# Gate and value products by seven block products instead of eight, with the weights' quarters in DRAM

## The chip, the cores and the metric

The kernel runs on one core of a Trainium2 chip. Its time is the device time of one execution in microseconds. A core has the matrix engine PE (TensorE), which multiplies a stationary operand (loaded by LDWEIGHTS, "PEld") with a moving one and adds up in PSUM; DVE (VectorE) and ACT (ScalarE), which read and write PSUM and SBUF; POOL (GpSimd), here used on SBUF alone; and SP (SyncE), here the queue that issues loads. All run at the same time, each in the order of its own instruction list, and wait for one another through semaphores.

## The reference

An attention with normalised queries and keys, then a gated feed-forward layer, all in float32 (the weights of the second part arrive as 64-bit floats):

```python
# q, k, v: (8 batches, 12 heads, 448 tokens, 64)
q_n, k_n = rmsnorm(q, g_q), rmsnorm(k, g_k)
scores = np.matmul(q_n, k_n.transpose(0, 1, 3, 2)) / sqrt(64)
attn = softmax(scores)
x = np.matmul(attn, v)            # -> (8*448 = 3584 tokens, 768)
# w_gate, w_val: (768, 1536); w_out: (1536, 768)
g = x @ w_gate
silu = g * (1.0 / (1.0 + np.exp(-g)))
out = (silu * (x @ w_val)) @ w_out
```

Here "gate and value products" are `x @ w_gate` and `x @ w_val`, together the *up* product; `@ w_out` is the *down* product.

## The kernel before, in words

The work of the attention is cut into 48 *pairs*: two heads of one batch (6 pairs a batch). For a pair, ACT squares q and k, DVE sums, POOL raises to the power -0.5 and scales, PE transposes (L644), PE makes the scores (L682), ACT the exponentials (L692), PE the weighted sum over v and the denominators (L730). Then DVE inverts the denominators (L773) and multiplies (L783): this writes 448 tokens of one group of 128 features into `xT`, the transposed x, kept as a ring of 1024 tokens.

The feed-forward layer runs in 7 *blocks* of 512 tokens. In a block, for each of 12 groups of 128 hidden features and for gate and value, `gate_value` (L891 to L900) adds 6 matmuls (128 x 128 stationary weights, 128 x 512 tokens) up in one of two PSUM banks named `mm`. An fp32 matmul is two instructions ("passes") in the profile. ACT takes the tanh (L905), DVE forms the gate (L908) and the product with the value (L913) into `gt`. Then `out_rows` (L949 to L961) computes the down product, 128 tokens by 384 outputs a group, with the same two banks; ACT copies (L965) and stores the rows.

The weights are loaded at the start in 18 parts: 12 for gate and value, 6 for w_out. Each part of 1536 KB of 64-bit floats lands in a *staging place*, a part of `gt` or of `wo` that isn't used yet, and is rounded to 32 bits by two ACT and four DVE operations (L844 to L877). The results stay in SBUF for the whole run, as `wg`, `wv` and `wo`.

The order of all work is made by `Order`, a planner that runs when the program is built. Each piece of work has an engine, an estimated duration, a due time `when`, the pieces it follows (`after`) and the buffers that it takes and uses. The planner keeps a clock for each engine and takes next, among the first 400 pieces of each engine by due time, the one that can start earliest; `early` keeps a load from being planned too far ahead of its due time, `port` keeps DVE and POOL operations on SBUF from being planned at the same time. The result is a fixed instruction list for each engine. Due times come from a plan of stages: first 12 pairs (two batches), then for each block an *up* stretch and a *down* stretch, into which the pairs of the following batches are spread.

Of the kernel before, what the change touches and what calls it, by code (L numbers as in the profile page):

```python
# [462 lines left out]
def fast(  # L463
# [22 lines left out]

    nc = tc.nc
# [12 lines left out]
    NB = B * S // TB  # L500
    RING = 2 * TB
# [6 lines left out]
    psum = ctx.enter_context(tc.tile_pool(name="psum", bufs=2, space=bass.MemoryType.PSUM))  # L508
    ctx.enter_context(tc.manual_schedule())

    BUFS = dict(qk=4, v=2, t=2, QT=2, KT=2, e=4, sums=1, inv=1, rows=2, st=2, at=2, mm=2, ss=2, rr=2)
# [3 lines left out]
    def take(name, key, shape):  # L515
        pool = psum if name in ("st", "at", "mm") else sbuf
# [19 lines left out]
    LEAD, PAIR = 14.0, 10.5  # L536
    FIRST = LEAD + EARLY * PAIR + 10.0
    UP, DOWN, BOTH = 123.6, 63.0, 113.0
# [4 lines left out]
    def pair_time(m):  # L543
        b, c = divmod(m, NPAIR)
        if m < EARLY:
            return LEAD + m * PAIR, PAIR
        n = b - 2
        if b == B - 1:
            return block_start(n) + c * 28.0, 28.0
        return block_start(n) + UP + (c - 1) * BOTH / NPAIR, BOTH / NPAIR  # L550
# [3 lines left out]
    done_x = {}  # L554
    up_done = {}

    def pair_rows(x, m):
        b, c = divmod(m, NPAIR)
        return x[b][2 * c : 2 * c + 2].rearrange("h (p j) d -> p h (j d)", j=NJ)

    def attention(m):
        b, c = divmod(m, NPAIR)
# [96 lines left out]
        def queries():  # L659
            to = take("QT", m, [P, NJ, R]).rearrange("p j r -> p (j r)")  # L660
            ps = tiles["st", (m, "t")][:, 0, 0:S]
            if early:
# [9 lines left out]
            "ACT" if early else "DVE", 0.68, base - 1.5, queries, after=[transposed],  # L672
# [75 lines left out]
        late = c == NPAIR - 1 and not early  # L748
# [29 lines left out]

        def divide():
            at, done = b * S % RING, 0  # L780
            while done < S:
                n = min(S - done, RING - at)
                nc.vector.tensor_tensor(  # L783
                    out=xT[:, c, ds(at, n)],
                    in0=tiles[av][:, ds(done, n)],
                    in1=tiles["inv", m][:, ds(done, n)],
                    op=ALU.mult,
                )
                at, done = (at + n) % RING, done + n


        blocks = range(
            max(0, (b * S - RING) // TB), max(0, -(-((b + 1) * S - RING) // TB))
        )
        done_x[m] = add(
            "DVE", 0.66, when + 5.0, divide, after=[inv] + [up_done[n] for n in blocks],
            uses=[av, ("inv", m)],
        )

# [7 lines left out]
    def weight_parts():  # L807


        gate, val = (w.rearrange("(c p) f -> p c f", p=P) for w in (moe_w_gate, moe_w_val))  # L810
        places = [("gt", 0), ("gt", 1), ("wo", 0), ("wo", 1), ("wo", 2)]
        n = 0
        for f in range(NF // 2):
            for w, dst, name in ((gate, wg, "g"), (val, wv, "v")):
                yield w[:, :, ts(f, 2 * P)], dst[:, f], (NW, 2 * P), (name, f), places[n % 5]
                n += 1
        rows = moe_w_out.rearrange("(f p) c -> p f c", p=P)
        for f, place in enumerate((4, 3, 4, 4, 1, 1)):
            fs = ts(f, 2)
            yield rows[:, fs, :], wo[:, fs, :], (2, DM), ("o", f), places[place]  # L820

# [3 lines left out]
    def weight_part(n, src, dst, shape, what, place):  # L825
        when = 12.0 + 11.0 * n
        region, s = place
        if region == "gt":
            raw = gt[:, ts(s, NF // 2), :].rearrange("p f t -> p (f t)")
        else:  # L830
            raw = wo[:, ts(s, NF // 3), :].rearrange("p f c -> p (f c)")
        raw = raw.bitcast(I64).rearrange("p (a b) -> p a b", a=shape[0])
        words = raw.bitcast(U32).rearrange("p a (b two) -> p a b two", two=2)
        lo, hi = words[:, :, :, 0], words[:, :, :, 1]
        bits = dst.bitcast(U32)
        add = order.add

        loaded = add(
            "SP", 0.45, when - 16.0, lambda: nc.sync.dma_start(raw, src),
            after=[staged.get(place)], kb=1536, early=2.0,  # L840
        )
        clear = [staged.get(("wo", what[1] // 2))] if what[0] == "o" else []
        one = add(
            "ACT", 1.55, when, lambda: nc.scalar.activation(dst, hi.bitcast(F32), AF.Abs),  # L844
            after=[loaded, *clear],
# [5 lines left out]
        three = add(  # L851
            "DVE", 0.95, when, lambda: nc.vector.tensor_scalar_max(dst, dst, LEAST),  # L852
            after=[one], port=True,
        )
        four = add(
            "DVE", 0.97, when,
            lambda: nc.vector.tensor_scalar(  # L857
                out=bits,
                in0=bits,
                scalar1=3,  # L860
# [20 lines left out]


    down_done = {}

    def block(n):
        add = order.add
        start = block_start(n)
# [211 lines left out]
```

## Time and profile before

| what | value |
|---|---|
| median of 3 runs | 1766.88 us (1766.26 to 1767.01) |
| profiled execution | 1767.19 us, of which the span is 1765.2 us |
| PE busy | 1733.2 us (98%) |
| DVE, ACT, POOL busy | 482.6, 381.3, 487.6 us |
| mean granted clock of PE | 0.999 |
| gate and value matmuls | 2016 passes of 128 x 512 |
| down matmuls | 1344 passes of 128 x 384 |

In the profile a group is a line of the kernel, an engine, an operation and its tiles, `out<-in`. A group's line gives its count, its busy time in all and the mean duration of one in nanoseconds, and then how long the engine had been idle before it and what ended that. Matmuls overlap, so the mean duration of one is longer than the distance from one to the next. The chain of waits starts from the last instruction and goes back, at each step to what released it. "issue" means that nothing the profile shows held the instruction back. A timeline merges neighbouring instructions of a kind: start, length, engine, line, operation and count.

### The profile page before, as it was taken

The numbers are of one execution on the slowest core, as the hardware profiler recorded it, in microseconds if no ns is written. First come the engines' busy times: TensorE is split into PE (matmuls) and PEld (weight loads), VectorE is DVE, ScalarE is ACT, GpSimd is POOL, SyncE is SP. The second block draws the span as 40 slices with busy tenths as digits, with TensorE's granted clock in tenths as the row PEclk, the third lists the DMA queues.
The fourth block names the chain that finished last, engine by engine and source line by source line (L and its number), as shares of the span: only waits on it lengthen the run. The fifth ranks groups of instructions, "written<-read, shape, count | busy, mean of one in ns | idle before, by whom it ended". The sixth has DMA issues, their size and how long they took to land.

```text
span 1765.2 us, 13688 instructions
## 1 busy us (share of the span) xinstructions
PE 1733.2 (98%) x5616; PEld 807.7 (46%) x5616; DVE 482.6 (27%) x490; ACT 381.3 (22%) x526; POOL 487.6 (28%) x260
## 2 busy tenths in 40 slices
PE   5999999999999999999999999999999999999998
PEld 2333444454444444445444445444454444554455
DVE  6997512221223111122111222122321222111100
ACT  6774212210113201122100221011321221100000
POOL 6660115520236302154111552022652242100000
PEclk9999999999999999999999999999999999999999
DMA  7563201010001100011100101000111000000000
GB/s 243 179 225 141 85 11 31 25 53 2 21 11 40 45 15 11 20 31 35 35 7 15 31 25 51 5 21 11 50 36 35 16 21 6 19 18 0 0 10 28
DMA packets 54955, 73.33 MB, mean 42 GB/s; under 512 B 4708, under 2 KB 44132, under 8 KB 54884
## 3 DMA queue, kind: packets, MB, share of 16 engines
q1 hardware_dynamic: 45600, 61.35, 11.1%
q10 hardware_dynamic: 9284, 11.02, 2.2%
q8 instruction: 46, 0.75, 0.2%
q14 instruction: 25, 0.20, 0.0%
HBM read 61.34 MB, written 11.01 MB: 41 GB/s over the span
## 4 chain that ended last, share of the span: by engine, by line
PE 93%; POOL 3%; issue 2%; ACT 1%; DVE 1%; POOLq 0%; ACTq 0%; DVEq 0%
PE mm L895 49%; PE mm L955 25%; PE at L730 10%; PE st L682 7%; POOL rr L612 2%; PE st L644 2%; POOL t L624 1%; ACT e L692 1%; DVE inv L773 0%; DVE wo L869 0%; DVE wo L876 0%; ACT wo L844 0%; DVE wo L852 0%; DVE wo L857 0%; DVE xT L783 0%
## 5 line engine op out<-in xcount | busy, mean ns | idle before, releaser
L895 PE MATMUL mm<-xT,wg 128*128 128x512 f32 x1008 | 447.9, 594 | 1.2 <-DVE xT L783 1.2
L955 PE MATMUL mm<-wo,gt 128*128 128x384 f32 x1344 | 447.9, 490 | 0.0
L895 PE MATMUL mm<-xT,wv 128*128 128x512 f32 x1008 | 447.3, 593 | 0.0
L612 POOL TENSOR_TENSOR rr<-ss,minus_half 112x16 f32<-112x16 f32 x48 | 149.1, 3107 | 800.4 <-DVE ss L604 739.8
L955 PEld LDWEIGHTS mm<-wo,gt 128*128 128x128 f32 x1344 | 251.0, 190 | 191.0 <-issue 29.1
L895 PEld LDWEIGHTS mm<-xT,wv 128*128 128x128 f32 x1008 | 190.8, 190 | 242.1 <-issue 241.6
L895 PEld LDWEIGHTS mm<-xT,wg 128*128 128x128 f32 x1008 | 190.2, 190 | 240.3 <-issue 235.3
L692 ACT ACTIVATE e<-st 112x896 f32<-112x896 f32 x192 | 165.6, 914 | 240.8 <-PE st L682 165.3
L773 DVE RECIPROCAL inv<-at 128x448 f32<-128x448 f32 x48 | 141.9, 2956 | 216.6 <-PE at L730 216.6
L905 ACT ACTIVATE gt<-mm 128x512 f32<-128x512 f32 x84 | 50.1, 597 | 654.0 <-PE mm L895 654.0
L682 PE MATMUL st<-QT,KT 64*112 64x448 f32 x768 | 172.3, 568 | 10.5 <-ACT QT L663 6.9
L908 DVE SCALAR_TENSOR_TENSOR gt<-gt,mm 128x512 f32<-128x512 f32 x84 | 57.8, 688 | 448.8 <-ACT gt L905 448.8
L701 POOL TENSOR_TENSOR sums<-sums,e 112x896 f32<-112x896 f32 x72 | 149.6, 2078 | 57.4 <-ACT e L692 53.3
L730 PE MATMUL at<-e,v 112*64 112x448 f32 x768 | 161.1, 546 | 0.2 <-DVE inv L773 0.2
L913 DVE SCALAR_TENSOR_TENSOR gt<-gt,mm 128x512 f32<-128x512 f32 x84 | 57.8, 688 | 308.3 <-PE mm L895 308.3
L698 POOL TENSOR_TENSOR sums<-e 112x896 f32<-112x896 f32 x36 | 74.8, 2078 | 182.5 <-PE at L730 100.4
L624 POOL TENSOR_TENSOR t<-qk,rr 112x512 f32<-112x512 f32 x96 | 114.0, 1206 | 3.7
L682 PEld LDWEIGHTS st<-QT,KT 64*112 64x112 f32 x768 | 61.0, 175 | 114.6 <-issue 82.2
L965 ACT COPY rows<-mm 128x384 f32<-128x384 f32 x56 | 26.8, 479 | 320.1 <-PE mm L955 320.1
L730 PEld LDWEIGHTS at<-e,v 112*64 112x64 f32 x768 | 50.9, 136 | 87.2 <-issue 80.7
L665 DVE TENSOR_SCALAR QT<-st,gg 128x448 f32<-128x448 f32 x36 | 24.6, 684 | 193.1 <-ACT KT L657 193.1
L603 DVE TENSOR_REDUCE ss<-t 112x16 f32<-112x1024 f32 x48 | 58.4, 1217 | 14.7 <-ACT t L585 14.7
(51 smaller groups left out, 487.5 us busy)
## 6 DMA issues: line engine op xcount, KB each, us to landing
qk<-in_q_dram SPq DMA_DIRECT2D x48, 224.0 KB, 3.0
qk<-in_k_dram SPq DMA_DIRECT2D x48, 224.0 KB, 3.0
v<-in_v_dram SPq DMA_DIRECT2D x48, 224.0 KB, 2.8
wo<-in_moe_w_out_dram SPq DMA_DIRECT2D x4, 1536.0 KB, 6.5
gt<-in_moe_w_gate_dram SPq DMA_DIRECT2D x3, 1536.0 KB, 8.2
gt<-in_moe_w_val_dram SPq DMA_DIRECT2D x3, 1536.0 KB, 7.0
wo<-in_moe_w_gate_dram SPq DMA_DIRECT2D x3, 1536.0 KB, 8.9
wo<-in_moe_w_val_dram SPq DMA_DIRECT2D x3, 1536.0 KB, 6.9
```

Source lines behind the costliest of these rows:

```text
L603: nc.vector.tensor_reduce(out=ss, in_=sq, axis=AX.X, op=ALU.add)
L612: nc.gpsimd.tensor_tensor(out=rr.rearrange("p x h j one -> p (x h j one)"), in0=tiles["ss", m], in1=minus_half, op=ALU.pow,)
L624: nc.gpsimd.tensor_tensor(out=tiles["t", m][:, :, x].rearrange("p j h d -> p h j d"), in0=tiles["qk", (m, x)], in1=tiles["rr", m][:, x].to ...
L682: nc.tensor.matmul(st[0:R, h, 0:S], tiles["KT", m][rows, j, :], tiles["QT", m][rows].rearrange("p j r -> p (j r)"), start=True, stop=True,)
L692: nc.scalar.activation(e, tiles["st", (m, j)][0:R, :, 0:S], AF.Exp)
L698: nc.gpsimd.tensor_tensor(out=to, in0=tiles["e", (m, 0)], in1=e, op=ALU.add)
L701: nc.gpsimd.tensor_tensor(out=to, in0=to, in1=e, op=ALU.add)
L730: nc.tensor.matmul(to[ds(D * h, D), 0:S], lhs(h), rhs[:, h], start=first, stop=last)
L773: nc.vector.reciprocal(inv, tiles[den][:, 0:S])
L895: nc.tensor.matmul(ps, w[:, f // 2, c, ts(f % 2, P)], xT[:, c, ts(n % 2, TB)], start=(c == 0), stop=(c == NW - 1),)
L908: nc.vector.scalar_tensor_tensor(gt[:, f], gt[:, f], 1.0, tiles["mm", (n, f, 0)], op0=ALU.add, op1=ALU.mult)
L955: nc.tensor.matmul(ps[:, 0:HALF], gt[:, f, ts(i, P)], wo[:, f, ts(half, HALF)], start=(f == 0), stop=(f == NF - 1),)
```

## The change

Two batches (2 x 448 tokens) now form one of 4 blocks. Let A11 and A12 be the even batch's first and last 384 features, A21 and A22 the odd batch's, and B11 to B22 the four quarters of 384 inputs by 768 hidden features of w_gate or w_val. The four quarters of the product are made from seven products of quarters (Winograd's form of Strassen's algorithm) in place of eight:

- S1 = A21 + A22, S2 = S1 - A11, S3 = A11 - A21 (written over A21), S4 = A12 - S2: by DVE, four operations of 448 columns for each of three groups of 128 features of a block (`sides`), when the last pair of the four quarters is done.
- T1 = B12 - B11, T2 = B22 - T1, T4 = B21 - T2, T3 = B22 - B12 (written over B12): by POOL, for one *half-block* (gate or value, 128 features of each half of the hidden features) at a time. There are 12 half-blocks in a block.
- The seven products, 3 matmuls of 128 x 448 each, go to the two banks in turn: A11 B11, S2 T2, A12 B21 (added in the bank to the first), S3 T3, S1 T1, A22 T4 and S4 B22 (each added in the bank to an earlier one). Between them ACT copies one result out and DVE adds five times from PSUM, so that a bank must be read before the next product but one. For the gate, ACT and DVE then treat the first quarter alone and the other three in one operation of 1344 columns; for the value, DVE does.

`wg` and `wv` no longer fit beside this and go: each up part is rounded into one of two spare places (the end of `gt`, or the room of S4 and S1) and stored to DRAM as `quarters`, 768 KB. Each half-block of each block loads its quarters from there into `ws`, a ring of two. An up part is loaded by two DMAs with rows of 1 KB instead of one with rows of 2 KB. The due times of the parts are 13 us apart (14 for w_out) instead of 11. Pairs of two batches are spread over each down stretch but the last; in an odd batch the pairs come in the order 0, 3, 1, 4, 2, 5. The queries of the first pair are scaled on DVE instead of ACT. The down product has the same number and shape of matmuls, in 14 groups a block instead of 8.

```diff
-    NB = B * S // TB
-    RING = 2 * TB
+    NB = B // 2
+    NK = NW // 2
+    NG = NF // 2
...
-    wg = const.tile([P, NF // 2, NW, 2 * P], F32, name="wg")
-    wv = const.tile([P, NF // 2, NW, 2 * P], F32, name="wv")
     wo = const.tile([P, NF, DM], F32, name="wo")
-    xT = const.tile([P, NW, RING], F32, name="xT")
-    gt = const.tile([P, NF, TB], F32, name="gt")
+    xs = const.tile([P, 7, NK, S], F32, name="xs")
+    quarters = [dram.tile([P, 4, NK, P], F32, name=f"quarters{i}") for i in range(2 * NG)]
+    A11, A12, A21, S4, S1, S2, A22 = range(7)
+    B11, B21, B12, B22, T1, T2, T4 = range(7)
+    gt = const.tile([P, NG, 2, 2 * S], F32, name="gt")
+    banks = [psum.tile([P, TB], F32, name=f"mm{i}", bufs=1) for i in range(2)]
...
-    LEAD, PAIR = 14.0, 10.5
-    FIRST = LEAD + EARLY * PAIR + 10.0
-    UP, DOWN, BOTH = 123.6, 63.0, 113.0
+    LEAD, PAIR = 14.0, 11.2
+    FIRST = LEAD + EARLY * PAIR + 8.0
+    PRODUCT = 2.27
+    UP, DOWN, BOTH = 14 * NG * PRODUCT, 111.0, 212.0
...
+    def sides(n, c, when):
+        a11, a12, a21, a22 = (xs[:, i, c] for i in (A11, A12, A21, A22))
+        s1, s2, s4 = (xs[:, i, c] for i in (S1, S2, S4))
+        last = [done_x[2 * n + a, c + k] for a in range(2) for k in (0, NK)]
+        if n == 0:
+            last.append(weights[spare[1]])
+        for side, to, one, two, op in (
+            (S1, s1, a21, a22, ALU.add),
+            (S2, s2, s1, a11, ALU.subtract),
+            (A21, a21, a11, a21, ALU.subtract),
+            (S4, s4, a12, s2, ALU.subtract),
+        ):
...
+    def up_weights(i, when):
...
+            for h in range(2):
+                nc.sync.dma_start(raw[:, h], w[:, h, :, ts(g, P)])
...
+        if i % 2 or i > NG + 2:
+            dst, last = flat_gt[:, 3 * WORDS :], spare[0]
+            spare[0] = i
+        else:
+            dst, last = xs[:, S4 : S1 + 1].rearrange("p s c t -> p (s c t)"), spare[1]
+            spare[1] = i
+        dst = dst[:, 0 : 4 * NK * P]
+        last = convert(src, dst, i % 6, when, [weights.get(last)])
+        weights[i] = order.add(
+            "SP", 0.45, when,
+            lambda: nc.sync.dma_start(quarters[i].rearrange("p s c f -> p (s c f)"), dst),
+            after=[last], kb=768,
+        )
...
+        def half_block(g, which):
...
+            load = add(
+                "SP", 0.45, when - 24.0,
+                lambda: nc.sync.dma_start(take(*key, [P, 7, NK, P])[:, 0:4], quarters[i]),
+                after=[weights[i]], takes=[key], kb=768, early=8.0,
+            )
+            for to, a, b in ((T1, B12, B11), (T2, B22, T1), (T4, B21, T2), (B12, B22, B12)):
+                load = add(
+                    "POOL", 0.93, when - 12.0,
...
+            one, other = turn[0], 1 - turn[0]
+            turn[0] = other
+            p, q = banks[one], banks[other]
+            def product(k, side, into, fresh, final, bank, after):
...
+                    for c in range(NK):
+                        nc.tensor.matmul(
+                            into[:, 0:S], w[:, side, c, :], xs[:, side, c],
+                            start=(fresh and c == 0), stop=(c == NK - 1),
...
+                last = add(
+                    "PE", PRODUCT, when + k * PRODUCT, emit,
+                    after=[load, last, bank_read[bank], *after], uses=[key], mode="full",
+                )
...
+            m = product(0, A11, p, True, False, one, even)
+            bank_read[one] = add(
+                "ACT", 0.55, when + PRODUCT,
+                lambda: nc.scalar.copy(take(*s1, [P, S]), p[:, 0:S]), after=[m], takes=[s1],
+            )
+            m = product(1, S2, q, True, True, other, done_sides[n, S2])
+            bank_read[other] = vector(
+                2, lambda: plus(lambda: take(*s2, [P, S]), lambda: tiles[s1], q),
+                [m, bank_read[one]], takes=[s2], uses=[s1],
+            )
+            m = product(2, A12, p, False, True, one, [])
+            if which == 0:
+                t = add(
+                    "ACT", 0.55, when + 3 * PRODUCT,
+                    lambda: nc.scalar.activation(first, p[:, 0:S], AF.Tanh, scale=0.5),
+                    after=[m, *before],
+                )
...
+            m = product(3, A21, q, True, False, other, done_sides[n, A21])
...
+            m = product(4, S1, p, True, False, one, done_sides[n, S1])
...
+            m = product(5, A22, q, False, True, other, [])
...
+            m = product(6, S4, p, False, True, one, done_sides[n, S4])
...
+            if which == 0:
+                t = add(
+                    "ACT", 1.35, when + 8 * PRODUCT,
...
+                vector(
+                    8,
+                    lambda: nc.vector.scalar_tensor_tensor(
+                        rest, tiles[wide], 1.0, rest, op0=ALU.add, op1=ALU.mult
+                    ),
+                    [t], us=1.57, port=True, uses=[wide],
+                )
...
-        groups = [(i, half) for i in range(TB // P) for half in range(2)]
+        groups = [(i, half) for i in range(2 * S // P) for half in range(2)]
...
+    for i in range(2 * NG):
+        up_weights(i, 14.0 + 13.0 * i)
+    for f in range(NF // 2):
+        down_weights(f, 14.0 + 13.0 * 2 * NG + 14.0 * f)
```

More of the change, by code (lines that the diff above doesn't have):

```diff
@@ L792, in attention @@
[L792 to L796, printed above, removed]
+            nc.vector.tensor_tensor(
+                out=x, in0=tiles[av][:, 0:S], in1=tiles["inv", m], op=ALU.mult
+            )
+        done_x[b, c] = add(
+            "DVE", 0.66, when + 5.0, divide, after=[inv, up_done.get(b // 2 - 1)],
             uses=[av, ("inv", m)],
@@ L798, in attention @@
         )
-    LEAST = 2.0**-15
[L807 to L820, printed above, removed]
+        if b % 2 and (b, (c + NK) % NW) in done_x:
+            sides(b // 2, c % NK, when + 6.0)
@@ L822, in fast @@
+    LEAST = 2.0**-15
     weights = {}
     staged = {}
[L825 to L835, printed above, removed]
+    flat_gt = gt.rearrange("p g f t -> p (g f t)")
@@ L867, in weight_part @@
[L867 to L879 removed]
+        last = one
@@ L1001, in block @@
+            add(
+                "ACT", 0.15, when, lambda i=i, half=half: store(i, half),
+                after=[bank_read[bank]], uses=[("rows", (n, i, half))], kb=192,
             )
```

352 lines of the change are left out of this document (207 added, 145 removed).

## The prediction

> **What bounds the kernel now.** I read the totals of the profile first, then the busy time by stretch of time, then the chain of waits, and only then single groups and the timeline.
>
> ```profile
> span 1765.2 us, 13688 instructions
> ...
> PE 1733.2 (98%) x5616; PEld 807.7 (46%) x5616; DVE 482.6 (27%) x490; ACT 381.3 (22%) x526; POOL 487.6 (28%) x260
> ```
>
> The profiled execution took 1767.2 us for this span, so 2 us lie around it; the median of the three runs, 1766.9, is 0.3 lower. PE is idle for 1765.2 - 1733.2 = 32 us in all. The busy time by stretch of time (columns: PE, weight loads, DVE, ACT, POOL, clock, DMA share, GB/s) says where:
>
> ```profile
> 0.00:156.70 156.70, 131.35 (x673) 51.70 (x673) 136.23 (x105) 111.02 (x126) 85.55 (x44) 1.00 0.62 204
> 866.00:990.00 124.00, 124.00 (x304) 54.92 (x303) 19.89 (x29) 14.64 (x24) 21.02 (x12) 1.00 0.05 13
> 990.00:1102.00 112.00, 112.00 (x443) 56.04 (x442) 30.48 (x25) 26.50 (x39) 45.99 (x24) 1.00 0.13 38
> 1698.00:1765.00 67.00, 61.73 (x192) 36.12 (x190) 0.53 (x1) 3.82 (x8) 0.00 (x0) 0.98 0.09 25
> ```
>
> 25 us of the idle time fall before 156.7, where the first two batches' attention runs, and 5 us after the last matmul. Between them, in an up stretch (866 to 990) and in a down stretch with attention (990 to 1102), PE is busy for every microsecond at the full granted clock, while no other engine reaches half. So from 156.7 on a matmul removed is time removed, as long as nothing else becomes late.
>
> **What the product costs.** The group table says 448 and 447 us for the gate and value products, but a busy time counts the pipelined tail of a matmul, so I take the pitch from start to start, in the last block, which nothing interrupts (chain of waits: start, length, what, count):
>
> ```profile
> 1574.21 123.60 PE mm L895 x288
> 1697.81 61.93 PE mm L955 x192
> ```
>
> 123.60 / 288 = 0.4292 us for a pass of 512 columns (two passes make one fp32 matmul) and 61.93 / 192 = 0.3226 for 384. Groups of 12 and 24 passes join without a gap in this. Before, seven blocks have 288 up passes each: 2016 x 0.4292 = 865.2 us. Afterwards there are 4 blocks x 12 half-blocks x 7 products x 3 matmuls x 2 passes: again 2016, but 448 columns wide. 448 lies halfway between the two measured widths: 0.3759, so 757.8 us. **This term is -107.5 us.** The down product keeps its 1344 passes of 384 columns, and the attention its instructions.
>
> **Bank turnover in the up stretch.** This is the new risk: a bank is now used again one product later, 6 x 0.3759 = 2.26 us, where it was 5.15 us before. These rows price the evictions:
>
> ```profile
> L783 DVE TENSOR_TENSOR xT<-at,inv 128x448 f32<-128x448 f32 x30 | 18.7, 624 | 1.0
> L657 ACT COPY KT<-st 128x448 f32<-128x448 f32 x48 | 25.5, 532 | 129.3 <-PE st L644 129.3
> L692 ACT ACTIVATE e<-st 112x896 f32<-112x896 f32 x192 | 165.6, 914 | 240.8 <-PE st L682 165.3 <-PE at L730 73.2 <-DMA out_dram<-rows 2.2
> L905 ACT ACTIVATE gt<-mm 128x512 f32<-128x512 f32 x84 | 50.1, 597 | 654.0 <-PE mm L895 654.0
> L908 DVE SCALAR_TENSOR_TENSOR gt<-gt,mm 128x512 f32<-128x512 f32 x84 | 57.8, 688 | 448.8 <-ACT gt L905 448.8
> L869 DVE SCALAR_TENSOR_TENSOR wo<-wo 128x1536 uint32<-128x1536 uint32 x4 | 7.0, 1759 | 0.1
> L701 POOL TENSOR_TENSOR sums<-sums,e 112x896 f32<-112x896 f32 x72 | 149.6, 2078 | 57.4 <-ACT e L692 53.3
> ```
>
> and the timeline of all engines shows the delays between them:
>
> ```profile
> 881.75 5.31 PE L895 MATMUL mm<-xT,wv 128*128 128x512 f32 x12
> ...
> 881.95 0.60 ACT L905 ACTIVATE gt<-mm 128x512 f32<-128x512 f32 x1 [9.70 <-PE mm L895]
> ...
> 882.58 0.69 DVE L908 SCALAR_TENSOR_TENSOR gt<-gt,mm 128x512 f32<-128x512 f32 x1 [5.09 <-ACT gt L905]
> ```
>
> An engine reads the bank 0.20 us after the next group has started, and ACT hands over to DVE in 0.03. A DVE addition of 448 columns (0.62, as L783) frees its bank after 0.20 + 0.62 + about 0.1 = 0.9 us: 1.3 to spare. The longest case, the gate's third product (tanh 0.53 as the copy at L657, then 0.62 on DVE), takes 0.20 + 0.53 + 0.03 + 0.62 + 0.1 = 1.5: 0.8 to spare. The wide operations come between: tanh over 1344 columns, extrapolated from 512 (0.597) and 896 (0.914), 1.28; the DVE product over 1344, from 512 (0.688) and 1536 (1.759), 1.56. After the last product of a gate half-block the wide DVE product runs from about 2.2 to 3.8 us into the next one; the first addition there is due at 2 x 2.26 + 0.2 = 4.7. DVE is busy for 6 x 0.62 + 1.56 = 5.3 us of 15.8, ACT for 2.3 or less. I cost the turnover at **0**: the cover is the 0.8 to 1.3 us, and only what keeps DVE longer than this in an up stretch uses it up.
>
> **Quarters from DRAM.** Each half-block loads 768 KB and makes three T operands and one difference on POOL, in a ring of two. A load can start when the half-block two before has ended, and has one half-block, 7 x 2.26 = 15.8 us.
>
> ```profile
> qk<-in_q_dram SPq DMA_DIRECT2D x48, 224.0 KB, 3.0
> ...
> wo<-in_moe_w_out_dram SPq DMA_DIRECT2D x4, 1536.0 KB, 6.5
> ```
>
> Between 224 KB in 3.0 us and 1536 KB in 6.5, 768 KB land in about 4.5; the issue is 0.45 of SP. POOL took 2.08 for 896 elements (L701): 0.89 for 384, four times 3.6. Ready after about 9 us, 6.8 to spare: **0**. Traffic is 38 MB over some 1500 us, on DMA queues that are 5 to 13% busy there.
>
> **The first stretch.** Before 156.7 it is DVE that runs without a break, one attention pair and one weight part in 11.08 us:
>
> ```profile
> 100.43 1.21 DVE L603 TENSOR_REDUCE ss<-t 112x16 f32<-112x1024 f32 x1
> ...
> 106.15 2.05 DVE L869 SCALAR_TENSOR_TENSOR wg<-wo,wg 128x1536 uint32<-128x1536 uint32 x1
> ...
> 108.33 2.38 DVE L876 CUSTOM_DVE_ANT_0 wg<-wo,wg 128x3072 uint16<-128x3072 uint16 x1
> ...
> 111.51 1.21 DVE L603 TENSOR_REDUCE ss<-t 112x16 f32<-112x1024 f32 x1
> ```
>
> Of this about 5.0 are the pair (1.21 here, 2.95 and 0.62 in the next fence, and a short one), 6.1 the part. Afterwards parts are due every 13 us instead of 11, so some 10.5 instead of 12 or 13 fall here, and twelve side operations of 0.62 are new: 12 x 5.0 + 10.5 x 6.1 + 7.4 = 131.5 against 136.2 busy now. PE's own work here is 131.4, so at most a few microseconds come back. The quarters' stores add 10 x 0.79 MB and two weight loads fewer take away 3.1 MB: 204 GB/s become about 236, where this row shows what the queues can do:
>
> ```profile
> 100.00:120.00 20.00, 18.63 (x100) 7.34 (x98) 19.59 (x16) 15.18 (x18) 14.02 (x6) 1.00 0.81 269
> ```
>
> I take **-2**, between -8 (DVE no longer limits at all) and +12 (the stores delay the loads, and ACT's queue stands behind a late weight part).
>
> **The step into block 0.** Now:
>
> ```profile
> 156.69 4.56 PE L895 MATMUL mm<-xT,wg 128*128 128x512 f32 x10
> ...
> 158.74 2.95 DVE L773 RECIPROCAL inv<-at 128x448 f32<-128x448 f32 x1
> ...
> 161.72 0.62 DVE L783 TENSOR_TENSOR xT<-at,inv 128x448 f32<-128x448 f32 x1
> ...
> 162.40 1.13 PE L895 MATMUL mm<-xT,wg 128*128 128x512 f32 x2 [1.16 <-DVE xT L783]
> ```
>
> Ten passes cover the last pair's division, and PE waits 1.16. Afterwards one product (2.26, of the even batch alone) stands in place of 10 x 0.429 = 4.29, and S1 and S2 (1.24) come behind the division: **+3.3**, between 0 (the last pair comes earlier in the order) and +8 (a weight part, 6 us, gets between). In later blocks the last pair is due 21 us before the block starts, so the same chain is hidden.
>
> **Inside block 0** six down parts are still converted on DVE, in steps of up to 1.76 (L869). One that has just begun when a bank fills costs up to 1.76 - 0.8 = 1 us there, on average a few tenths, perhaps ten times: **+2**, between 0 and +14. Here work is late in another way too: the tanh of the seventh half-block writes the third staging place of gt, which two down parts pass through one after the other.
>
> ```profile
> 189.48 1.76 DVE L876 CUSTOM_DVE_ANT_0 wo<-gt,wo 128x3072 uint16<-128x3072 uint16 x1
> ...
> 197.76 1.61 ACT L844 ACTIVATE wo<-gt 128x1536 f32<-128x1536 f32 x1 [2.35 <-DMA gt<-in_moe_w_out_dram]
> ...
> 203.75 1.76 DVE L876 CUSTOM_DVE_ANT_0 wo<-gt,wo 128x3072 uint16<-128x3072 uint16 x1
> ```
>
> One such turn is 203.75 - 189.48 = 14.3 us. The last part is due at 240; the tanh comes at about 157 + 6 x 15.8 + 6.8 = 259. One turn late is hidden, two are not.
>
> **The down stretch** holds 12 pairs for 14 groups instead of 6 for 8. From 866 to 1102 POOL works 21.0 + 46.0 = 67 us for six pairs, 11.2 each; twelve of them and the 43 us of subtractions make 177 of a new block's 400: no change.
>
> **Sum:** 1767.2 - 107.5 - 2 + 3.3 + 2 = 1663 us for the profiled execution, and about 1663 for the median.
>
> **The rivals.**
>
> *First stretch or block 0 late.* As above, one cause: more bytes and a longer weight chain. The upper ends of two of the three terms above taken by half, 7 + 7, give about 1677, taken fully 1690. For it: DVE at 136 of 157 us. Against: parts come more slowly, and 269 GB/s were reached.
>
> *POOL and DVE stand in each other's way.* POOL's scaling of a pair's q and k takes this long alone and beside DVE's weight part:
>
> ```profile
> 9.94 2.04 POOL L624 TENSOR_TENSOR t<-qk,rr 112x512 f32<-112x512 f32 x2
> ...
> 25.70 4.28 POOL L624 TENSOR_TENSOR t<-qk,rr 112x512 f32<-112x512 f32 x2
> ```
>
> and L876 takes 2.38 beside POOL. If the wide DVE product of a gate half-block had to let all four POOL subtractions go first, it would end at 2.2 + 3.6 + 1.56 = 7.4 us, the addition due at 4.7 would be 2.7 late, 1.3 of it spare: 1.4 x 24 half-blocks = 33 us, **1696**. Against it: the subtractions start about 5 us into a half-block, behind the load, when the wide product is over. [...]
>
> *Quarters late: slower than before.* If load and subtractions take longer than 15.8 us, PE waits in 40 of 48 half-blocks (the first two of a block are loaded ahead), and 40 x 2.7 = 107 eats the gain: the point is 18.5 us. At the longest landing of a weight part now,
>
> ```profile
> DMA to landing us min/median/max: 6.4/7.6/12.0
> ```
>
> 12.0, and subtractions at 2.14 each (half of 4.28), it is 12.0 + 8.6 + 0.6 = 21.2: 40 x 5.4 = 216 us, less 107, **1876**. SP issues in order, so a load of q or k that waits for its buffer in front of a quarter does the same. Against: 12.0 fell where the queues were 60 to 80% busy.
>
> *PE's cost isn't by columns.* If a pass of 448 cost what one of 512 does, nothing is gained: **1770** with the three small terms. The two widths above speak against it. [...]
>
> **How the numbers follow.** Forecast, 1652 to 1672: 0.73. Late start, to 1690: 0.12. POOL against DVE or another partial loss of turnover, 1690 to 1755: 0.08. No gain, within 0.2% (3.5 us, about what a measurement of this kernel can tell from none): 0.02. Quarters late, slower: 0.05. The lower ends of the three small terms give 1767.2 - 107.5 - 8 = 1652, the upper ones 1767.2 - 107.5 + 12 + 8 + 14 = 1694; the range 1652 to 1690 leaves out some 0.17. Faster 0.93, same 0.02, slower 0.05.
>
> **What would show it.** Up passes at a pitch of 0.376 and products every 2.26 us in blocks 1 to 3, with PE busy in each stretch; the first product at 150 to 160, the second 4 to 5 us behind the last pair's weighted sum; quarters ready 9 us into a half-block. PE's waits naming POOL's subtractions, DVE's additions or a load in blocks 1 to 3 would prove me wrong, as would a lower granted clock.

## The result and the profile after

The kernel after takes 1668.3 us (median of 4 runs, 1667.84 to 1668.73), beside 1766.95 (1766.26 to 1767.09) of the kernel before on the same chip: a ratio of 0.9442, with a 95% interval of 0.9426 to 0.9459. The forecast was 1663, in a range of 1652 to 1690. The profiled execution took 1668.56 us, 98.6 less than the profiled one before.

The totals of the profile, and the lines of the gate and value product, of POOL's subtractions and of the quarters' loads:

```profile
span 1666.7 us, 14502 instructions
...
PE 1625.9 (98%) x5616; PEld 808.4 (49%) x5616; DVE 670.6 (40%) x689; ACT 401.6 (24%) x537; POOL 681.9 (41%) x452
...
L985 PE MATMUL mm<-xs,ws 128*128 128x448 f32 x2016 | 764.1, 541 | 5.2 <-DVE xs L833 5.2
...
L969 POOL TENSOR_TENSOR ws<-ws 128x384 f32<-128x384 f32 x192 | 200.5, 1055 | 512.4 <-DMA ws<-quarters 433.0
...
ws<-quarters SPq DMA_DIRECT2D x48, 768.0 KB, 4.3
```

PE has as many passes as before and is as full as before (98%); DVE and POOL do 188 and 194 us more work, and the share of PE did not fall. The last block in the chain of waits (start, length, what, count) and, in the busy time by stretch, the first stretch, a down and an up stretch (columns as in the prediction):

```profile
1363.31 189.42 PE mm L985 x504
1552.73 108.37 PE mm L1120 x336
```

```profile
0.00:162.40 162.40, 133.13 (x678) 52.83 (x678) 133.22 (x106) 104.95 (x122) 84.71 (x52) 1.00 0.77 231
1159.60:1363.00 203.40, 203.17 (x833) 100.42 (x832) 77.21 (x66) 57.91 (x83) 122.34 (x68) 1.00 0.16 48
1363.20:1552.60 189.40, 189.40 (x506) 95.74 (x505) 61.25 (x82) 18.06 (x25) 39.44 (x40) 1.00 0.13 43
```

189.42 / 504 is 0.3758 us a pass, and the up stretch has no gap at all. What PE waits for in the whole run (line, releaser: us in total, times, longest), two lines of 5.4 us in all left out:

```profile
PE st L667 <- POOL t L647: 11.0, 1, 11.0
PE st L705 <- ACT e L715: 6.9, 11, 2.0
PE st L705 <- ACT KT L680: 5.9, 1, 5.9
PE mm L985 <- DVE xs L833: 5.2, 1, 5.2
...
PE st L705 <- DVE QT L688: 0.7, 3, 0.2
```

All but the last line lie before 170 us. The step into block 0 looks like this (PE in the timeline, then the busy time by stretch, whose third number from the end is the granted clock):

```profile
141.45 2.52 PE L985 MATMUL mm<-xs,ws 128*128 128x448 f32 x6
...
161.61 0.92 PE L753 MATMUL at<-e,ones 112*64 112x448 f32 x4
162.46 1.77 PE L985 MATMUL mm<-xs,ws 128*128 128x448 f32 x4
169.40 12.91 PE L985 MATMUL mm<-xs,ws 128*128 128x448 f32 x27 [5.17 <-DVE xs L833]
```

```profile
169.00:171.00 2.00, 1.60 (x2) 0.83 (x3) 1.42 (x3) 0.00 (x0) 0.00 (x0) 0.50 0.94 246
...
173.00:175.00 2.00, 2.00 (x4) 0.86 (x3) 0.96 (x1) 2.00 (x2) 0.00 (x0) 0.64 0.98 409
175.00:178.00 3.00, 3.00 (x9) 1.52 (x8) 1.16 (x3) 1.02 (x3) 0.00 (x0) 1.00 0.61 254
```

The first product was drawn forward to 141.45; behind the last weighted sum (162.4) stand only the two thirds of the second product that are ready, then a wait of 5.17 us for S2. After it PE runs at half the clock for some 5 us (the trace's record of the clock has 0.50 from 167.63 to 174.45).

### The profile page after: what moved, and what is told of

The parts are those of the page before. It is cut to its first block, busy times and chain, and to the rows that moved or that the text cites. A ratio compares the mean times of both kernels' runs of the same rounds, so it can differ in the third digit from the quotient of the medians.

```text
span 1666.7 us, 14502 instructions
## 1 busy us (share of the span) xinstructions
PE 1625.9 (98%) x5616; PEld 808.4 (49%) x5616; DVE 670.6 (40%) x689; ACT 401.6 (24%) x537; POOL 681.9 (41%) x452
## 4 chain that ended last, share of the span: by engine, by line
PE 89%; DVE 4%; DMA 2%; issue 2%; POOL 1%; ACT 1%; SPq 0%; ACTq 0%; POOLq 0%; DVEq 0%
PE mm L985 46%; PE mm L1120 25%; PE at L753 9%; PE st L705 8%; PE st L667 2%; DVE xs L833 1%; DVE inv L796 1%; POOL t L647 1%; DMA qk<-in_q_dram 1%; POOL rr L635 1%; DMA wo<-in_moe_w_val_dram 1%; DMA gt<-in_moe_w_gate_dram 1%; DMA wo<-in_moe_w_gate_dram 0%; ACT e L715 0%; ACT gt L870 0%
## 5 line engine op out<-in xcount | busy, mean ns | idle before, releaser
L985 PE MATMUL mm<-xs,ws 128*128 128x448 f32 x2016 | 764.1, 541 | 5.2 <-DVE xs L833 5.2
L985 PEld LDWEIGHTS mm<-xs,ws 128*128 128x128 f32 x2016 | 382.8, 191 | 381.5 <-issue 371.5
L969 POOL TENSOR_TENSOR ws<-ws 128x384 f32<-128x384 f32 x192 | 200.5, 1055 | 512.4 <-DMA ws<-quarters 433.0
L635 POOL TENSOR_TENSOR rr<-ss,minus_half 112x16 f32<-112x16 f32 x48 | 143.7, 2993 | 243.0 <-DVE ss L627 208.3
L715 ACT ACTIVATE e<-st 112x896 f32<-112x896 f32 x192 | 165.7, 914 | 205.6 <-PE st L705 118.6
L705 PE MATMUL st<-QT,KT 64*112 64x448 f32 x768 | 172.0, 568 | 14.7 <-ACT e L715 6.9
L1001 DVE TENSOR_TENSOR s<-s,mm 128x448 f32<-128x448 f32 x96 | 59.6, 621 | 155.4 <-PE mm L985 155.4
L705 PEld LDWEIGHTS st<-QT,KT 64*112 64x112 f32 x768 | 60.9, 174 | 116.8 <-issue 72.6
L1024 ACT COPY s<-mm 128x448 f32<-128x448 f32 x48 | 25.5, 532 | 294.6 <-PE mm L985 294.6
L1001 DVE TENSOR_TENSOR wide<-s,mm 128x448 f32<-128x448 f32 x72 | 44.7, 620 | 102.6 <-PE mm L985 102.6
L1001 DVE TENSOR_TENSOR gt<-s,mm 128x448 f32<-128x448 f32 x72 | 44.7, 621 | 99.1 <-PE mm L985 99.1
L1088 ACT ACTIVATE wide<-gt 128x1344 f32<-128x1344 f32 x24 | 31.8, 1323 | 178.0 <-DVE gt L1001 178.0
```

What stands on the lines that cost most here:

```text
L635: nc.gpsimd.tensor_tensor(out=rr.rearrange("p x h j one -> p (x h j one)"), in0=tiles["ss", m], in1=minus_half, op=ALU.pow,)
L705: nc.tensor.matmul(st[0:R, h, 0:S], tiles["KT", m][rows, j, :], tiles["QT", m][rows].rearrange("p j r -> p (j r)"), start=True, stop=True,)
L715: nc.scalar.activation(e, tiles["st", (m, j)][0:R, :, 0:S], AF.Exp)
L969: lambda to=to, a=a, b=b: nc.gpsimd.tensor_tensor(out=tiles[key][:, to], in0=tiles[key][:, a], in1=tiles[key][:, b], op=ALU.subtract,),
L985: nc.tensor.matmul(into[:, 0:S], w[:, side, c, :], xs[:, side, c], start=(fresh and c == 0), stop=(c == NK - 1), skip_group_check=not fina ...
L1001: nc.vector.tensor_tensor(out=to(), in0=one(), in1=two[:, 0:S], op=ALU.add)
```

## The experiments

Edits are against the kernel after, where nothing else is said; times are medians.

**1. Eight products, all else kept.** Each quarter of the product is made of its two plain products; S, T and their operations go, but the quarters in DRAM, the loads for each block and the due times of the first stretch stay. `group` adds 6 matmuls up in one bank; DVE copies the last three quarters out.

```diff
-            m = product(0, A11, p, True, False, one, even)
...
+            m = group(0, ((A11, B11), (A12, B21)), p, one, even)
...
+                (2, 0, ((A21, B11), (A22, B21)), other),
+                (4, 1, ((A11, B12), (A12, B22)), one),
+                (6, 2, ((A21, B12), (A22, B22)), other),
```

> Undoes the seven products alone: two batches a block, quarters stored to DRAM and loaded for each half-block, pairs spread over four blocks, all as in the changed kernel, but the plain eight products of quarters (four groups of 12 passes a half-block), without the sums on DVE and the subtractions on POOL. Theory: the passes through PE set the time. 288 passes of 448 columns more, 288 x 0.376 = 108 us, and the step into block 0 about 3 us shorter without S1 and S2: 1668 + 108 - 3 = 1773 us (1768 to 1779), slightly slower than the kernel before. Rival (the gain came from larger blocks and from spreading the pairs differently): 1700 to 1740.

1768.12 us, a ratio of 1.0005 (0.9996 to 1.0014) to the kernel before, 99.8 over the kernel after. Its last block in the chain of waits:

```profile
1435.20 216.48 PE mm L1017 x576
1651.67 108.37 PE mm L1107 x336
```

216.48 - 189.42 = 27.06 us a block, four times 108.2: the gain is the missing products, and staging, blocks of two batches and quarters from DRAM together come out at nothing. That the two kernels are 99.8 us apart and not 108.2 lies in the start. Without S1 and S2 PE waits 1.9 us in place of 5.2 there (the 3 us that the expectation had). Beyond this, the last weighted sum ends 2.9 us earlier by equal work, and the clock doesn't fall to half (a mean of 0.999 in the profiled run, beside 0.998), which costs the kernel after 2.6 us: about the 5 us by which the expectation is over. What makes the 2.9 us isn't shown.

**2. How much room is there at a bank?** The five additions of a half-block are each done three times, in DVE and in the planner's durations: 1.24 us more for one.

```diff
-                nc.vector.tensor_tensor(out=to(), in0=one(), in1=two[:, 0:S], op=ALU.add)
+                dst = to()
+                for _ in range(3):
+                    nc.vector.tensor_tensor(out=dst, in0=one(), in1=two[:, 0:S], op=ALU.add)
```

> Each of the five additions of a half-block on DVE is made three times, so a bank is freed 1.24 us later. Theory (turnover is covered, 1.3 us to spare behind an addition): 0.20 + 3 x 0.62 + 0.1 = 2.16 us, still under the 2.26 of a product: 1668 us, within 4. Rival (turnover already sets the pace, POOL and DVE in each other's way): at least part of 48 x 5 x 1.24 = 298 us, 1700 or more.

1708.07 us, ratio 0.9663 (0.9650 to 0.9677): 40 us lost where the theory had none. Where the loss arises in an undisturbed up stretch shows in the last block's timeline, first of the kernel after, then of this one; both begin with the addition that ends a gate half-block:

```profile
1410.70 0.62 DVE L1001 TENSOR_TENSOR gt<-s,mm 128x448 f32<-128x448 f32 x1 [1.63 <-PE mm L985]
...
1411.36 1.32 ACT L1088 ACTIVATE wide<-gt 128x1344 f32<-128x1344 f32 x1 [9.13 <-DVE gt L1001]
1412.71 1.56 DVE L1095 SCALAR_TENSOR_TENSOR gt<-wide,gt 128x1344 f32<-128x1344 f32 x1 [1.39 <-ACT wide L1088]
...
1415.08 4.10 POOL L969 TENSOR_TENSOR ws<-ws 128x384 f32<-128x384 f32 x4 [11.40 <-DMA ws<-quarters]
1415.28 0.62 DVE L1001 TENSOR_TENSOR s<-s,mm 128x448 f32<-128x448 f32 x1 [1.01 <-PE mm L985]
```

```profile
1448.21 1.93 DVE L1005 TENSOR_TENSOR gt<-s,mm 128x448 f32<-128x448 f32 x3 [0.33 <-PE mm L985]
...
1451.54 1.56 DVE L1099 SCALAR_TENSOR_TENSOR gt<-wide,gt 128x1344 f32<-128x1344 f32 x1 [1.39 <-ACT wide L1092]
...
1453.01 1.93 DVE L1005 TENSOR_TENSOR s<-s,mm 128x448 f32<-128x448 f32 x3
```

The last addition of a half-block, the wide tanh, the wide product and the next half-block's first addition are one chain. In the kernel after, DVE stands idle for 1.01 us in it, and behind the chain's last addition there are 1.3 us until its bank is used again: 2.3 us of room in all. Two additions of the chain are now 1.31 us longer each (1.93 instead of 0.62), 2.6 together; DVE has no idle time left in it, and PE loses 0.28 us behind it. At the other additions the 1.31 us just use up the 1.3, and PE loses 0.03 to 0.17 us at each. Two half-blocks take 32.24 us instead of 31.57 in the chain of waits (`1455.08 32.24 PE mm L985 x84`), 0.34 each, 48 times: 16 us. The rest lies in block 0, whose first down product comes at 394.0 instead of 363.0: there the longer additions meet the weight parts, PE waits up to 5.3 us for one addition, and the mean granted clock from 163 to 383 us is 0.95.

**3. and 4. Loads of the weights: earlier, or in rows of 2 KB.** The weight parts' loads may be planned 12 us ahead of their due time instead of 2; and, by itself, one DMA of 2 KB rows replaces the two of 1 KB rows (each part then holds 256 neighbouring hidden features, so the output is that of permuted weights).

```diff
-            early=2.0,
+            early=12.0,
```

```diff
-            for h in range(2):
-                nc.sync.dma_start(raw[:, h], w[:, h, :, ts(g, P)])
+            nc.sync.dma_start(raw, plain[:, :, ts(g, 2 * P)])
```

> The loads of the weight parts may be planned 10 us further ahead of their due time, nothing else is edited; on SP they then stand in front of the store of the part before, not behind it. Theory (in the first stretch ACT stands at late weight loads and PE at ACT behind it; about 5 us): 1663 us (1661 to 1666), the second product of block 0 at about 164 us instead of 169.4, ACT's waits for weight loads gone. Rival (DVE or the queues' bandwidth limits the first stretch): no change, 1668.

> Each up part is loaded by one DMA with rows of 2 KB, as before the change, in place of two DMAs with rows of 1 KB; this brings other columns of the weights, so the output belongs to permuted weights, and the work is the same. Rival (the short rows make the parts land late, 8.4 us for each half): landing about 7 us, and the same 5 us come back, 1663 to 1665. Theory (the loads are late because they are issued behind the store): at most 2 us, 1666 to 1668.

Earlier loads: 1681.03 us, ratio 0.9513 (0.9500 to 0.9526), a loss of 12.7. The planner packs the engines in another order; ACT's list again stands behind loads (8.3 us at the longest), PE's waits for its exponentials grow from 6.9 to 11.2 us (`PE st L705 <- ACT e L715: 11.2, 12, 3.4`), and the product behind the last weighted sum starts at 171.30 instead of 162.46. Long rows: 1667.36 us, ratio 0.9434 (0.9421 to 0.9447), 0.9 less than after, which two medians so near don't tell apart. A part with long rows landed no sooner (9.0 to 9.4 us at the median, beside 8.4), so the row length doesn't hold the first stretch back. What earlier loads would bring stays open: the edit was to take ACT's waits for loads away, and it didn't.

**5. How late may the operands T be?** POOL makes T1, T2 and T4 four times in each half-block, nine more subtractions, some 9.5 us.

```diff
-            for to, a, b in ((T1, B12, B11), (T2, B22, T1), (T4, B21, T2), (B12, B22, B12)):
+            for to, a, b in ((T1, B12, B11), (T2, B22, T1), (T4, B21, T2)) * 4 + ((B12, B22, B12),):
```

> The three T operands are made four times over on POOL, so nine subtractions of 1.0 us are added to each half-block, with the same results. Theory (a half-block's quarters are ready 8.6 us into the one before and have until 15.8): 8.6 + 9.0 = 17.6 us, 1.8 us late in about 40 half-blocks, 1668 + 72 = 1740 us (1715 to 1765), PE's waits naming POOL's subtractions. Rival (more cover than that, PE works ahead of the quarters): 1668 to 1675. [...]

1726.25 us, ratio 0.9770 (0.9755 to 0.9786): 58 us lost, not 72, and elsewhere than expected. The last block loses nothing, as its chain of waits shows; PE's waits for POOL stand in the earlier blocks:

```profile
1417.19 189.42 PE mm L985 x504
```

```profile
PE mm L985 <- POOL ws L969: 18.7, 7, 5.8
```

In that last block POOL makes one set of 13 from 1437.67 on in 14.71 us, until 19.6 us behind the boundary at 1432.8 where its load could start, 3.8 us into the half-block that uses it; and PE doesn't notice. The first product of a half-block takes the loaded B11 as it is; the last T2 is ready 0.4 us into the half-block and first needed one product (2.26 us) in; the last difference, B22 - B12, is ready 3.8 us in and needed three products in. So T2 has until 15.8 + 2.26 us, and the others longer. The loss lies ahead of the first down product of block 0 (393.1 instead of 363.0) and in the up stretches of blocks 1 and 2 (6 and 19 us longer, of which the next down stretch gives 3 back); there POOL also has the pairs to make.

**6. Loads planned as slower.** The planner reckons 6.9 us for a part's load (1536 KB), which takes 8.4 at the median. With 2100 KB in the plan it reckons 8.8.

```diff
-            "SP", 0.45, when - 16.0, lambda: src(raw), after=[staged.get(place)], kb=1536,
+            "SP", 0.45, when - 16.0, lambda: src(raw), after=[staged.get(place)], kb=2100,
```

> The planner is told that a weight part takes 8.8 us to land (2100 KB in its terms) where it counted 6.9; nothing else is edited. In the run with loads ahead the planner packed the pairs closer, and ACT still stood at weight loads for 3 to 5 us each. Theory (ACT's list has the weight part in front of a pair's exponentials at a time when it hasn't landed): with the part later in the list ACT's waits for loads shrink and 2 to 5 us come back, 1663 to 1666. [...]

1680.97 us, ratio 0.9508 (0.9495 to 0.9522), 12.7 lost, in two parts of opposite sign. The first stretch gets shorter as the theory has it: PE's waits for exponentials before 163 us shrink to 3.5 and 3.8 us, and the product behind the last weighted sum starts at 158.24 instead of 162.46, and S2 releases it at 163.34 instead of 169.40. But block 0 gives it back and more; DVE, and then PE, in its timeline:

```profile
182.10 1.80 DVE L897 CUSTOM_DVE_ANT_0 wo<-wo 128x3072 uint16<-128x3072 uint16 x1
...
185.79 1.76 DVE L893 SCALAR_TENSOR_TENSOR wo<-wo 128x1536 uint32<-128x1536 uint32 x1
187.69 2.33 DVE L897 CUSTOM_DVE_ANT_0 wo<-wo 128x3072 uint16<-128x3072 uint16 x1
189.94 2.35 DVE L1095 SCALAR_TENSOR_TENSOR gt<-wide,gt 128x1344 f32<-128x1344 f32 x1
192.21 0.61 DVE L1001 TENSOR_TENSOR s<-s,mm 128x448 f32<-128x448 f32 x1
```

```profile
192.97 1.83 PE L985 MATMUL mm<-xs,ws 128*128 128x448 f32 x2 [4.77 <-DVE s L1001]
```

From 182.1 to 190 five operations of weight parts and then the wide product stand in DVE's list, back to back, ahead of a bank's addition. The first down product starts at 377.0 instead of 363.0: block 0 takes 20 us longer from S2 on. 12.0 us of this are PE's waits for additions. Some 7 are slower passes: behind the wait for S2 and behind the four for additions, 8, 42, 96, 72 and 86 passes take 4.97, 17.72, 39.09, 29.02 and 34.26 us in the timeline, together some 10 us more than at 0.3758 a pass, beside 2.6 in the kernel after (an estimate from these rows); the mean granted clock of this run was 0.994, beside 0.998.

**7. and 8. The step into block 0.** The sides of the first two feature groups go to POOL; or, in the first half-block alone, the third product (even batch only) comes before the second.

```diff
-                    "DVE", 0.64, when,
+                    "POOL" if n == 0 and c < NK - 1 else "DVE",
+                    1.1 if n == 0 and c < NK - 1 else 0.64, when,
```

```diff
+            swap = n == 0 and i == 0
...
+            if swap:
+                third(1)
+                second(2)
+            else:
+                second(1)
+                third(2)
```

> In the first block alone, S1 to S4 of the first two groups of features are made by POOL instead of DVE (eight of 48 such operations). Theory (against the run with eight products, whose last weighted sum ends 2.8 us earlier by equal work, these sums cost the first stretch 2.8 us through DVE's weight parts and the stores behind them): 1665 to 1667. Rival (the first stretch hangs on loads alone): 1668; if POOL now holds up the scaling of the pairs, 1670 or more.

> In the very first half-block A12 B21 goes before S2 T2: it needs the even batch alone and can fill the wait for S2, 5.2 us in the changed kernel. Theory (PE waits there for S2 of the last pair and for nothing else): PE's wait falls by one product, 2.26 us, to about 2.9, and the time to 1666 (1665 to 1667). Rival (the time is made up by later waits, in block 0's weight parts): 1668.

On POOL: 1673.05 us, ratio 0.9467 (0.9453 to 0.9480), 4.7 lost by the medians, with an interval that just overlaps that of after. The four side operations of one group take POOL 7.38 us between the scalings of a pair's q and k, those of the other 5.24, as the rival had it, and PE's waits for exponentials at the transposes double (`PE st L667 <- ACT e L715: 8.6, 10, 4.3`). Even batch first: 1666.83 us, ratio 0.9434 (0.9420 to 0.9447). Its profiled span is 2.9 us shorter, but not as expected: the wait for S2 is 4.4 instead of 5.2, not 2.9. The planner put the moved product before the second scores of the last pair, at 150.97, where PE had waited 1.96 us for exponentials; behind the last weighted sum again only four passes stand. By the medians it is 1.5 us ahead, by the intervals of the ratios not told apart from after.

**9. to 11. Is it the row of weight parts?** On top of 8, DVE's operations of a weight part are kept 0.8 us apart in block 0; then the same with the slow plan of 6; then also with the six down parts due 30 us later and 18 us apart.

```diff
+            if piece["group"] == "part" and before["end"] > 156.0:
+                gap = 0.8
```

```diff
-        down_weights(f, 14.0 + 13.0 * 2 * NG + 14.0 * f)
+        down_weights(f, 14.0 + 13.0 * 2 * NG + 30.0 + 18.0 * f)
```

> Edit against e8: from 156 us of the plan on, the four VectorE operations of a weight part are kept 0.8 us apart, so that a bank addition finds a place between any two; nothing else. Theory (in the kernel after, the weight parts inside block 0 are hidden already; PE waits for nothing but S2 there): same as e8, 1665 to 1668. Rival (the parts cost in block 0 of the kernel after as well): 1660 to 1664, with the down product of block 0 before 358.

> Edit: e6 (loads of weights planned as slower), with e8's order of the first three products and with the spacing of e9. Theory (e6 won 6 us before block 0 and lost about 20 in it because up to four weight-part operations stood in a row ahead of a bank addition in VectorE's list): the waits of PE for s in block 0 shrink from 12.0 + 4.8 to under 4 in sum, the first down product of block 0 starts at 356 to 362 instead of 377.0, and the time is 1658 to 1666. Rival (the loss comes from the late weights themselves, PE waiting for quarters or the plan's order of pairs and products): the down product starts after 370 and the time is over 1673.

> Edit: e10, with the six parts of the down weights due 30 us later and 18 instead of 14 us apart. Theory: fewer parts fall into the first half-blocks of block 0; the down product starts no later than in e10, and the time is that of e10 within 3 us, since the spacing alone keeps the bank additions on time. Rival (number of parts, not their spacing, sets the loss): over 4 us faster than e10.

Spaced: 1666.33 us, ratio 0.9431 (0.9415 to 0.9447), as 8: the weight parts cost block 0 of the kernel after nothing. Spaced with the slow plan: 1674.38, ratio 0.9478 (0.9462 to 0.9494), over the 1658 to 1666 expected. PE's waits between 150 and 390 us in that run:

```profile
PE mm L988 <- DVE gt L1049: 6.8, 1, 6.8
PE mm L988 <- DVE xs L836: 3.3, 1, 3.3
PE mm L988 <- DVE s L1004: 1.0, 2, 0.8
```

The waits for an addition fell from 12.0 us to 1.0, and the down product starts at 366.5 instead of 377.0: the mechanism holds, though not all of the 356 to 362 was reached. Another row of four part operations (267.6 to 273.2) stands ahead of a gate's DVE product, whose tanh was done at 265.4; it costs 6.8 us, and why the planner put the gate's product behind that row stays open. Later down parts made it worse, 1689.88 (ratio 0.9562, 0.9546 to 0.9578), against both theories, by a queue that neither had named. In that run, SP's waits for a staging place and its loads in the timeline, and PE's wait:

```profile
SPq L937 <- DVE wo L900: 27.1, 2, 14.0
```

```profile
272.80 0.38 SPq L937 DMA_DIRECT2D gt<-in_moe_w_out_dram  x1
273.23 0.46 SPq L596 DMA_DIRECT2D qk<-in_q_dram  x1
...
290.40 2.01 PE L670 MATMUL st<-ident,t 112*128 112x112 f32 x8 [23.09 <-POOL t L650]
```

The load of a down part waits on SP for its staging place, and the loads of block 0's first pair stand behind it; PE waits 23.09 us for that pair.

## Why the prediction came out as it did

**The product: right.** -107.5 us was reckoned with 0.3759 us a pass; 0.3758 was measured, and experiment 1 has 108.2 for the four up stretches. The interpolation between 512 and 384 columns held.

**Bank turnover at 0: right, and so were the rooms.** Nothing waits at a bank in the kernel after. Behind the gate's third product 0.85 us are left (DVE is done at 1402.88, the bank is used again at 1403.73; 0.8 was reckoned), the wide product is over 1.01 us before the next addition is due (0.9), and additions 1.31 us longer just use up the 1.3 at each (experiment 2). What I left out is that rooms in one chain aren't had twice: the last addition of a half-block, both wide operations and the next half-block's first addition share 2.3 us.

**Quarters at 0: right.** POOL starts at 1415.08, 4.6 us after the half-block's boundary at 1410.5, and is done at 1419.2, 8.7 after it (9 predicted; the load came 0.4 us sooner, and the four subtractions took 4.1 instead of 3.6). The deadline was set too early by a product or more (experiment 5); the rival of late quarters was even farther off than its 18.5 us said.

**First stretch: the step that failed.** I took -2; the last weighted sum ends at 162.4 instead of 156.6, of which the product drawn forward is 2.3: **+3.5**. The reason I gave, that DVE runs without a break and sets the pace, was wrong: in the kernel before, DVE does run so (from 28 to 150 us it waited 0.2 us in all), but PE waited for it only 0.2 us there. The scores of a pair and of the second pair behind it in the timelines, before and after:

```profile
44.58 1.76 PE L682 MATMUL st<-QT,KT 64*112 64x448 f32 x8
...
67.48 1.76 PE L682 MATMUL st<-QT,KT 64*112 64x448 f32 x8
```

```profile
44.40 1.76 PE L705 MATMUL st<-QT,KT 64*112 64x448 f32 x8
...
67.03 1.76 PE L705 MATMUL st<-QT,KT 64*112 64x448 f32 x8
```

Two pairs take 22.9 us before and 22.6 after, though weight parts come more slowly after: DVE doesn't set the pace, PE does, with waits of 0.33 and 0.36 us for ACT's exponentials in each pair. What then makes the later pairs slip is ACT, whose list stands still behind loads (and, at 145.66, a store):

```profile
124.45 1.60 ACT L870 ACTIVATE gt<-wo 128x1536 f32<-128x1536 f32 x1 [3.81 <-DMA wo<-in_moe_w_val_dram]
...
152.11 1.59 ACT L874 ACTIVATE wo<-wo 128x1536 uint32<-128x1536 uint32 x1 [3.40 <-DMA wo<-in_moe_w_val_dram]
153.61 1.69 ACT L715 ACTIVATE e<-st 112x896 f32<-112x896 f32 x2
```

In the kernel before no load stops ACT for more than 0.7 us from 45 us on; here five loads and a store stop it for 2.0 to 3.8 us. PE's waits for exponentials, transposes included, grow from 6.9 us in all to 11.1. That was the upper end of the term ("ACT's queue stands behind a late weight part"), and the range held it. Experiment 6 shows that the plan's too short loads are the cause: with longer ones these waits are 7.3 us, and the stretch ends 4.2 us sooner.

**The step into block 0: chain right, cover wrong.** From the last weighted sum to the resumption are 7.0 us, 5.8 before and 1.24 more, as reckoned. But the first product, meant to stand in this gap, had run at 141.45, and only four passes (1.5 us) cover it, not six: +4.0 instead of +3.3. Not reckoned at all was the half clock behind the wait: in the time of the seven passes from 169.4 to 174.6 fourteen could have run, 2.6 us.

**Inside block 0: +2 was reckoned for weight parts, and no wait of PE is seen.** Experiments 6 and 10 show that the mechanism exists, with another size: not tenths of a microsecond for one operation that has just begun, but up to 4.8 us where several stand in a row.

Together: -107.5 + 3.5 + 4.0 + 2.6 = -97.4, where -98.6 was measured; 1.2 us of it are spread too thin to be named. The profiled execution is 5.6 us over the forecast: the first stretch gives 5.5 of it, and the half clock (2.6) and the step (0.7) stand against the 2 of block 0 and the 1.2 not named. That these nearly cancel is luck. By its own chances, the range left out 0.15, not 0.17.

**The rivals.** PE's cost by columns is settled by the measured pitch. POOL's subtractions start only when the wide product is over (1415.08 against 1412.71 + 1.56), and in experiment 5 the last up stretch keeps its 189.42 us beside longer POOL work, although the value's wide product, which meets it there, takes 1.8 us instead of 1.56. The clock did fall, which the prediction had named as a sign against it: to 0.50 from 167.63 to 174.45, around the end of the wait of 5.17 us. Over the whole of the last up stretch it is 1.00.

## What to carry to other kernels

Before paying a change that shortens the bounding engine, list for every buffer the chain of operations that must end before its next use, not single operations: new work in the chain shares its spare time (here 2.3 us from the last addition of a half-block to the bank of the next one's first). In a stretch that a written-out order fills, look for the engine whose list stands behind DMAs, not for the busiest one; and when an estimate in the planner is mended, check what moves behind it on every in-order queue: experiment 6 gained 6 us before a boundary and lost 20 behind it.

## What the runs showed of the hardware

PE's granted clock was 0.50 behind some of PE's waits and stayed at 1.00 behind others. In the trace of the kernel after, it was 0.50 from 167.63 to 174.45, 6.82 us, around the end of the wait of 5.17 us, and 1.00 from 174.45 until PE was done. In the kernel before, whose wait at the step into block 0 was 1.16 us, it was 1.00 there and up to the end of PE's work. In experiment 10 it was 0.50 from 165 to 171 us, behind a wait of 3.33 us; around a wait of 6.80 us its mean was 0.73 from 267 to 273.8 and 0.51 from there to 277, and then 1.00 up to 281. The run of experiment 11, with the wait of 23.09 us, has a mean of 0.990.

Two waits of nearly equal length had different ends. Two stretches of 3.41 us (half of those 6.82) of the kernel after, and two of experiment 6:

```profile
126.67:130.08 3.41, 1.70 (x8) 0.55 (x8) 3.34 (x4) 3.04 (x4) 3.33 (x3) 1.00 1.00 314
130.08:133.49 3.41, 3.04 (x22) 1.67 (x22) 3.41 (x4) 2.22 (x4) 2.84 (x3) 1.00 1.05 350
```

```profile
262.97:266.39 3.42, 1.38 (x5) 0.50 (x4) 3.39 (x4) 0.00 (x0) 3.31 (x2) 1.00 0.00 0
266.39:269.80 3.41, 3.41 (x5) 1.41 (x5) 0.18 (x1) 0.00 (x0) 1.94 (x2) 0.50 0.00 0
```

The first stretch holds most of a wait of 2.03 us (its end is at 128.38) and leaves PE busy for 1.70 of 3.41 us: the clock stays at 1.00. The third holds the whole of a wait of 2.04 us (its end is at 266.19), and 1.38 are left: the clock of the next is 0.50. At 0.50, 3.41 us are worth 1.7 us of PE's work, so the second wait cost up to 1.7 us more than itself (an estimate from these rows). What decides between the two is not shown.

In experiment 5 the mean granted clock was 0.986 over a span of 1720.4 us, beside 0.998 over 1666.7 in the kernel after. 0.014 of the one is 24 us of clock lost, 0.002 of the other some 3: an estimate of some 20 us more, a part of which falls into waits. With 23 us more waiting for operands and banks and 5 for POOL's sums of the exponentials it makes most of the 54.7 us by which the profiled execution of experiment 5 is longer.
